# Gated linear attention and a multiplicative FFN: state, scores and values of the last sixteen chunks in one block of 64x64 quarters

## The chip, the cores and the metric

The kernel runs on one core of a Trainium2 chip. The metric is the device time of one execution in microseconds, the median of several runs. All data is float32; TensorE also uses the fp32r form of it, on operands that are split into several parts.

## The reference

An attention layer with a gated state runs over 4 x 8 sequences (batch x heads) of 768 steps with head dimension 48. Its result, laid out as 3072 tokens x 384, goes through a feed-forward network with two factors.

```python
for t in range(S):
    state = alpha[:, :, t, :, None] * state + np.einsum('bhd,bhe->bhde', k[:, :, t], v[:, :, t])
    y[:, :, t] = np.einsum('bhd,bhde->bhe', q[:, :, t], state)
...
x = np.ascontiguousarray(attn_out.transpose(0, 2, 1, 3)).reshape(B * S, H * D)
a = x @ w1            # 384 x 1024
b = x @ w2            # 384 x 1024
h = a * b @ w3        # 1024 x 1024
return (h @ w_out)    # 1024 x 384
```

## The kernel before

**Tiling.** The 3072 tokens are 24 chunks of C = 128, six per sequence (NCH), with all eight heads of a batch entry in one chunk. Heads go in NP = 4 pairs: head 2j lies on partitions 0 to 63 and head 2j + 1 on 64 to 127 (i is 0 or 1; DP = 64 with 48 used). The decays are taken into k and q by sums of logarithms (L324 to L359), so that inside a chunk the scores are plain products. Three chunks (G) make a token group, whose result xd[g] is written to DRAM, read back and multiplied with the FFN weights.

**One chunk.** `transposed` (L370) turns k and q of a chunk on TensorE and ScalarE copies them to qkT (L383). `scores` forms k times q, 128 keys x 128 queries per head, and VectorE masks them with a bitwise and (ms). `attend_state` (L463) multiplies the state T with q into two PSUM banks y; `attend` (L477) adds the values times ms and ScalarE copies y to x (L489), which two DMA transfers write to xd. `outer` (L386) makes the state's new term k times v, `advance` (L405) rescales the state on POOL every second chunk.

**The late chunks.** From chunk TURNED = 8 on, `turned_scores` (L422) leaves out the quarter of each score block that is all masked: keys 0 to 63 for all 128 queries (L430, 128 columns), keys 64 to 127 for queries 64 to 127 (L430, 64 columns), each on 48 rows and 64 columns of the array. For odd heads (i = 1) the two key halves come to lie on exchanged partitions, and `turn_v` (L164) makes POOL copy their values to vt in that order, with the key halves exchanged. Four VectorE instructions mask a chunk (L440). The value products are split: `attend_low` (L415) handles queries 0 to 63 from keys 0 to 63, 64x64 quarters of the array placed between the next chunk's scores, and L482 handles queries 64 to 127 from all 128 keys, after the next chunk's transposes. In scores and y each row half of the array writes a bank of its own.

**Order.** The loop at L689 runs over the chunks: in iteration n stand the state products of chunk n - 1, the scores of chunk n with the low value products of n - 1, the transposes of n + 1, then the masks, the value products of n - 1, the outer products of n, and pieces of the FFN's first stage (`gate`, L515 by way of `exact`). From iteration 9 on an iteration has 3, 3, 2 or no such pieces. The iterations without pieces (9, 13, 17, 21) split the x of a token group into three parts (`split_x`, L507 to L509). Instructions are placed by a scheduling layer; `issue_after` marks hold some of them behind others. Each engine runs its own in its order. PSUM has eight banks, all from one pool (`bank`), which gives out the bank that was given back first.

**Queues.** SP issues the loads of alpha (L147), k and q (L153, L154), v (L159), the weights (L236), and the stores of x (L305) and of the gates (L590). At the head of an iteration `store` empties the list of x transfers, and then come the loads of later chunks: alpha of n + 5, k and q of n + 4, v of n + 2. POOL issues the small transfers of the decays.

After the 24 chunks come the remaining FFN products, the weights w3 times w_out, and the last projection.

Of the kernel before, what the change touches and what calls it, by code (L numbers as in the profile page):

```python
# [48 lines left out]
def kernel(  # L49
# [31 lines left out]
    TURNED = 8  # L81
    assert D <= DP and DM % C == 0 and DF % CW == 0 and S % C == 0 and N % G == 0
# [81 lines left out]
    def turn_v(n):  # L164
        if turned(n):
            for half in range(2):
                nc.gpsimd.tensor_copy(out=vts[n % 2][ds(DP * half, DP), :, 0:D],
                                      in_=st["v", n][ds(DP * (1 - half), DP), 1::2, 0:D])
# [39 lines left out]
    for half in range(2):  # L208
        nc.gpsimd.tensor_copy(out=keep_turned[ds(DP * half, DP), 1 - half], in_=keep[ds(DP * half, DP), ds(DP * half, DP)])
    nc.gpsimd.memset(keep_turned[DP:, 1], -1)  # L210
# [204 lines left out]
    def attend_low(n, jj, i, half):  # L415

        s, w = ds(DP * i, DP), (vts[n % 2] if i else st["v", n])
        h = half * NP // 2 + jj
        nc.tensor.matmul(st["y", n][0][i][ds(DP * half, DP), jj, 0:DP], w[s, h if i else 2 * h, :],  # L419
                         st["ms", n][s, i, h, 0:DP], start=(n % NCH == 0 and jj == 0), stop=True, skip_group_check=True)  # L420

    def turned_scores(n):  # L422

        qkT = st["qkT", n]
        sc = [bank().rearrange("p (j c) -> p j c", j=NP) for _ in range(2)]
        for j in range(NP):
            for part in range(2):
                for i in range(2):
                    r, t = ds(DP * i, D), slice(DP * part, C)
                    nc.tensor.matmul(sc[i][ds(DP * (part ^ i), DP), j, t], qkT[r, 0, j, ds(DP * part, DP)],  # L430
                                     qkT[r, 1, j, t], start=True, stop=True)
            if turned(n - 1):
                for i in range(2):
                    attend_low(n - 1, j % 2, i, i ^ (j < 2))
        ms = work.tile([C, 2, NP, C], FP32, tag="ms", name="ms")
        for i in range(2):
            r = ds(DP * i, DP)
            low, high = (keep_turned[r, 0], keep_turned[:, 1]) if i else (keep[r, 0:DP], keep[:, DP:])
            for x, mask, t in ((slice(DP * i, DP * (i + 1)), low, slice(0, DP)), (slice(0, C), high, slice(DP, C))):
                masked = nc.vector.tensor_tensor(ms[x, i, :, t].bitcast(I32), sc[i][x, :, t].bitcast(I32),  # L440
                                                 mask[:, None, :].to_broadcast([x.stop - x.start, NP, DP]),
                                                 op=ALU.bitwise_and)
        ends_of_part1[0] = mark["ms", n] = masked.ins
        st["ms", n] = ms

    def scores(n):
        if turned(n):
            return turned_scores(n)
# [28 lines left out]
    def attend(n):  # L477
        (y, heads), ms, vc = st.pop(("y", n)), st.pop(("ms", n)), st.pop(("v", n))
        for j, i, to in heads:
            if turned(n):  # L480
                w = vts[n % 2][:, j, :] if i else vc[:, 2 * j, :]
                nc.tensor.matmul(to[:, DP:], w, ms[:, i, j, DP:], start=False,  # L482
                                 stop=(j % HP == HP - 1), skip_group_check=True)
            else:
                nc.tensor.matmul(to, vc[:, 2 * j + i, :], ms[:, i, j, :], start=(n % NCH == 0 and j % HP == 0),  # L485
                                 stop=(j % HP == HP - 1), skip_group_check=True)
# [202 lines left out]
    for n in range(N + 1):  # L689
# [17 lines left out]
        if n:  # L707
            attend_state(n - 1)
# [168 lines left out]
```

## Time and profile before

| | |
|---|---|
| median of 3 runs | 465.62 us (464.9 to 467.0) |
| profiled execution | 464.49 us, its span 462.8 us |
| granted TensorE clock | 1.00 |
| PE busy in the span | 446.9 us, 97% |
| DVE (VectorE) busy | 371.7 us, 80% |
| ACT (ScalarE) busy | 276.4 us, 60% |
| POOL busy | 95.1 us, 21% |
| state products L474 | 320 records, 13.3 us |
| scores of late chunks L430 | 512 records, 34.8 us in two forms |
| low value products L419 | 256 records, 32.8 us in two forms |
| high value products L482 | 256 records, 17.4 us in two forms |

The span is what the profiler saw of the execution; the profiled execution's own time lies 1.7 us above it. Busy times of TensorE are those of overlapping records, whose ends are modelled; the start times of successive groups say more. A float32 matmul is two records of PE and two of PEld (weight load). Late chunks are on TensorE from 67.7 to 184.6 us.

A line of a timeline has start in us, length in us, engine, source line, operation, the tile written and the tiles read, rows x columns of the array in use, the shape of the moving operand, the number of records and, in brackets, the idle time before it with the engine that ended it. A line of a table of groups has the busy time in us and the mean of one in ns, then the idle time before. A line of a table of stages has the window, its length, and for each of PE, PEld, DVE, ACT and POOL the busy time and number of instructions, then the granted clock, the DMA share and GB/s.

### The profile page before, as it was taken

Reading aid. Unit: us, or ns where it says so; the run is one execution under the profiler, and the core shown is the slowest. Engines: PE = TensorE matmul, PEld = TensorE weight load, DVE = VectorE, ACT = ScalarE, POOL = GpSimd, SP = SyncE. Lnnn points to the kernel's source line nnn. Section 1 sums busy time; section 2 is a strip of 40 time slices with the busy share of each in tenths; the row PEclk is TensorE's granted clock in tenths of the full one; section 3 lists DMA queues with packets and bytes.
Section 4 is the critical chain, followed back from the end, with each engine's and each line's share of the span. In section 5 each row is a group of like instructions: output and inputs, shape, how many; then the busy total and the mean of one; then the engine's idle time right before and its main releaser. Section 6 shows DMA issues by size and latency. Waiting matters only on the chain.

```text
span 462.8 us, 11150 instructions
## 1 busy us (share of the span) xinstructions
PE 446.9 (97%) x4296; PEld 423.2 (91%) x4296; DVE 371.7 (80%) x610; ACT 276.4 (60%) x544; POOL 95.1 (21%) x186
## 2 busy tenths in 40 slices
PE   4998999999999999999999999999999999999996
PEld 2675699898999989999999999999999999999996
DVE  2779997999979988999998999997542967776671
ACT  4685975767658563988875676764545443333430
POOL 6234232325414430121221201212010000000000
PEclk9999999999999999999999999999999999999999
DMA  9999999999999974466856446412115875665511
GB/s 173 254 208 228 261 224 192 248 209 219 184 227 193 234 165 138 130 224 212 235 178 196 146 128 177 149 52 86 51 48 153 243 210 180 186 178 159 166 51 52
DMA packets 148869, 80.37 MB, mean 174 GB/s; under 512 B 97392, under 2 KB 138608, under 8 KB 148816
## 3 DMA queue, kind: packets, MB, share of 16 engines
q1 hardware_dynamic: 143040, 64.44, 57.3%
q0 software_dynamic: 5776, 15.22, 11.0%
q8 instruction: 34, 0.56, 0.5%
q14 instruction: 19, 0.16, 0.1%
HBM read 57.58 MB, written 22.06 MB: 172 GB/s over the span
## 4 chain that ended last, share of the span: by engine, by line
PE 88%; DVE 4%; DMA 4%; ACT 2%; issue 1%; SPq 0%; DVEq 0%; ACTq 0%
PE bank L515 72%; DMA kq<-in_q_dram 3%; PE bank L381 3%; PE bank L430 3%; PE bank L482 2%; PE bank L474 2%; PE bank L340 1%; PE bank L393 1%; PE bank L346 1%; PE bank L454 1%; PE bank L343 1%; PE bank L419 1%; DVE qk L359 1%; DVE ms L457 1%; PE bank L485 1%
## 5 line engine op out<-in xcount | busy, mean ns | idle before, releaser
L515 PE MATMUL bank<-x,w 128*128 128x384 f32 x1152 | 210.2, 337 | 1.7 <-ACT qkT L383 1.1
L515 PEld LDWEIGHTS bank<-x,w 128*128 128x128 f32 x1152 | 200.2, 188 | 4.1 <-ACT qkT L383 1.4
L515 PE MATMUL bank<-w3o,ab 128*128 128x384 f32 x576 | 100.2, 336 | 0.0
L515 PEld LDWEIGHTS bank<-w3o,ab 128*128 128x128 f32 x576 | 99.9, 188 | 0.0
L540 ACT ACTIVATE bank<-bank 128x384 f32<-128x384 f32 x96 | 45.6, 476 | 43.4 <-PE bank L515 43.1
L524 ACT ACTIVATE t<-bank 128x384 f32<-128x384 f32 x64 | 31.9, 499 | 54.9 <-PE bank L515 54.9
L590 POOL DMA_DIRECT2D abd<-ab x45 | 25.8, 573 | 137.9 <-DVE ab L576 121.3
L383 ACT COPY qkT<-bank 128x512 f32<-128x512 f32 x48 | 26.2, 596 | 24.8 <-PE bank L381 24.8
L641 DVE TENSOR_TENSOR ab<-abl,ab 128x1024 fp32r<-128x1024 f32 x24 | 29.3, 1223 | 12.3 <-ACT ab L640 12.3
L640 ACT ACTIVATE ab<-abl 128x1024 fp32r<-128x1024 f32 x24 | 25.5, 1061 | 20.2 <-PE bank L515 18.4
L515 PE MATMUL bank<-wo,w3T 128*128 128x384 f32 x192 | 35.9, 334 | 0.0
L576 DVE TENSOR_TENSOR ab<-bank,r 128x384 f32<-128x384 f32 x44 | 24.1, 548 | 12.5 <-PE bank L515 6.3
L515 PEld LDWEIGHTS bank<-wo,w3T 128*128 128x128 f32 x192 | 33.5, 188 | 0.0
L249 ACT ACTIVATE power<-power,rebias 128x512 uint32<-128x512 uint32 (+1 forms) x36 | 25.3, 701 | 12.6 <-DVE power L248 12.4
L359 DVE TENSOR_TENSOR qk<-kq,e 128x768 f32<-128x768 f32 x24 | 23.1, 964 | 11.3 <-ACT e L350 7.9
L526 DVE SCALAR_TENSOR_TENSOR o<-bank,t 128x384 f32<-128x384 f32 x24 | 13.4, 557 | 23.0 <-issue 13.7
L642 DVE SCALAR_TENSOR_TENSOR ab<-ab,abl 128x1024 fp32r<-128x1024 f32 x24 | 29.2, 1217 | 0.0
L526 DVE SCALAR_TENSOR_TENSOR r<-bank,t 128x384 f32<-128x384 f32 x40 | 22.0, 550 | 6.8 <-PE bank L515 3.4
L251 DVE SCALAR_TENSOR_TENSOR mant<-mant,rest 128x512 f32<-128x512 uint32 (+1 forms) x36 | 23.4, 649 | 3.7 <-ACT rest L244 3.7
L252 DVE SCALAR_TENSOR_TENSOR power<-raw,power 128x512 uint32<-128x512 uint32 (+1 forms) x36 | 23.5, 653 | 2.4 <-ACT power L249 2.4
L253 DVE TENSOR_TENSOR mant<-mant,power 128x512 f32<-128x512 f32 (+1 forms) x36 | 23.6, 655 | 0.5
L244 ACT ACTIVATE rest<-raw 128x512 f32<-128x512 uint32 (+1 forms) x36 | 23.3, 649 | 0.0
(102 smaller groups left out, 675.2 us busy)
## 6 DMA issues: line engine op xcount, KB each, us to landing
abl<-abd SPq DMA_DIRECT2D x24, 512.0 KB, 4.7
abd<-ab POOLq DMA_DIRECT2D x45, 192.0 KB, 3.2
raw<-in_moe_w_dram SPq DMA_DIRECT2D x64, 128.0 KB, 3.4
raw<-in_moe_w_dram SPq DMA_DIRECT2D x12, 512.0 KB, 5.8
xT<-xd POOLq DMA_DIRECT2D x9, 576.0 KB, 4.7
kq<-in_k_dram SPq DMA_DIRECT2D x24, 192.0 KB, 5.2
kq<-in_q_dram SPq DMA_DIRECT2D x24, 192.0 KB, 5.4
xd<-x SPq DMA_DIRECT2D x48, 96.0 KB, 3.9
```

What stands on the lines that cost most here:

```text
L249: nc.scalar.activation(power, power, AF.Relu, scale=2.0 ** 23, bias=rebias)
L359: mark["qk", n] = nc.vector.tensor_mul(qks[n % 3][:, :, :, 0:D], st.pop(("kq", n)), st.pop(("e", n)).rearrange("p i (h d) -> p i h d", h=H ...
L383: mark["qkT", n] = nc.scalar.copy(qkT[:, :, :, ds(DP * half, DP)], tp[half]).ins
L515: nc.tensor.matmul(p, w[part][i], x[part][i], start=start and part == parts[0] and i == 0, stop=stop and part == parts[-1] and i == n - 1, ...
L524: nc.scalar.activation(t, p1, AF.Copy, scale=(1.0 + 1.0 / P) * scale)
L526: nc.vector.scalar_tensor_tensor(to, p2, scale, t, op0=ALU.mult, op1=ALU.add)
L540: nc.scalar.activation(p, p, AF.Copy, scale=1.0 + 1.0 / P)
L576: nc.vector.tensor_mul(ab, p, r[0])
L590: (nc.gpsimd if late else nc.sync).dma_start(out=abd[g][:, f, :], in_=ab)
L640: nc.scalar.activation(t[:, 0], ab, AF.Copy, scale=1.0 - 2.0 ** -13)
L641: nc.vector.tensor_sub(t[:, 1], ab, t[:, 0].bitcast(FP32))
L642: nc.vector.scalar_tensor_tensor(t[:, 2], t[:, 0].bitcast(FP32), -1.0 - 1.0 / P, ab, op0=ALU.mult, op1=ALU.add)
```

## The change

For chunks 8 to 23, state, scores and values are put on 64x64 quarters of the array and issued as one block.

- `attention(n)` takes the place of `attend_state(n - 1)` and `turned_scores(n)` at the head of an iteration and merges two lists by the number of columns issued so far. One holds chunk n - 1's state and value products of head pairs 0 to 2 (LQ = 3), on the quarters whose row half and column half differ. The other holds chunk n's scores and then the products of pair 3 of chunk n - 1, on the quarters whose halves agree.
- The scores of both heads of a pair go to the same bank, on the partitions of their half: one bank for keys 0 to 63 and one half-filled for keys 64 to 127. Two masks with 128 partitions take the place of four.
- All value products of chunk n - 1 lie in that block, in three parts per pair (state, keys 0 to 63 for all queries, keys 64 to 127 for queries 64 to 127), so that L482 falls away for these chunks. The value halves that `turn_v` copies are chosen accordingly: its two copies now take even and odd heads.
- y is one bank of 3 x 128 columns and one of 128. Two ScalarE copies of that size take them to x, at the place where `attend` stood; in the scheduled order they now stand ahead of the qkT copies. Four DMA transfers per chunk write x in place of two, of the same bytes in all.
- Chunks 0 to 7 keep their code. Iteration 8 still takes the state of chunk 7 by `attend_state` and its values by `attend`, with the new scores of chunk 8; iteration 24 has the block without scores.

```diff
     TURNED = 8
+    LQ = 3
...
     def turn_v(n):
         if turned(n):
-            for half in range(2):
-                nc.gpsimd.tensor_copy(out=vts[n % 2][ds(DP * half, DP), :, 0:D],
-                                      in_=st["v", n][ds(DP * (1 - half), DP), 1::2, 0:D])
+            for i in range(2):
+                nc.gpsimd.tensor_copy(out=vts[n % 2][ds(DP * i, DP), :, 0:D],
+                                      in_=st["v", n][ds(DP * (1 - i), DP), i::2, 0:D])
 
...
-    for half in range(2):
-        nc.gpsimd.tensor_copy(out=keep_turned[ds(DP * half, DP), 1 - half], in_=keep[ds(DP * half, DP), ds(DP * half, DP)])
-    nc.gpsimd.memset(keep_turned[DP:, 1], -1)
+    for i in range(2):
+        nc.gpsimd.tensor_copy(out=keep_turned[ds(DP * i, DP), 0], in_=keep[ds(DP * i, DP), ds(DP * i, DP)])
+    nc.gpsimd.memset(keep_turned[:, 1], -1)
+    keeps = [keep_turned[:, 0:x, None, :].to_broadcast([C, x, NP, DP]) for x in (1, 2)]
...
-    def attend_low(n, jj, i, half):
-
-        s, w = ds(DP * i, DP), (vts[n % 2] if i else st["v", n])
-        h = half * NP // 2 + jj
-        nc.tensor.matmul(st["y", n][0][i][ds(DP * half, DP), jj, 0:DP], w[s, h if i else 2 * h, :],
-                         st["ms", n][s, i, h, 0:DP], start=(n % NCH == 0 and jj == 0), stop=True, skip_group_check=True)
-
-    def turned_scores(n):
-
+    def quarters(n):
+
+        ms, vc, vt, qkT = st.pop(("ms", n)), st.pop(("v", n)), vts[n % 2], st.pop(("qkT", n))
+        y = [bank()[:, 0:x * C].rearrange("p (j c) -> p j c", c=C) for x in (LQ, NP - LQ)]
+        first, state = set(), n % NCH > 0
+
+        def add(j, i, w, x, t):
+            at = j >= LQ
+            to = y[at][ds(DP * (i if at else 1 - i), DP), j - LQ * at, t]
+            nc.tensor.matmul(to, w, x, start=(at, i) not in first, stop=True, skip_group_check=True)
+            first.add((at, i))
+
+        def steps(heads):
+            for j in heads * state:
+                yield 2, [(j, i, Ts[n % 2][ds(DP * i, D), j, :], qkT[ds(DP * i, D), 1, j, :], slice(0, C)) for i in range(2)]
+            for j in heads:
+                yield 2, [(j, i, vt[DP:, j, :] if i else vc[0:DP, 2 * j, :], ms[ds(DP * i, DP), 0:2, j, :], slice(0, C))
+                          for i in range(2)]
+            for j in heads:
+                yield 1, [(j, i, vc[DP:, 2 * j + 1, :] if i else vt[0:DP, j, :], ms[ds(DP * i, DP), 2, j, :], slice(DP, C))
+                          for i in range(2)]
+
+        def act(x):
+            for y in x:
+                add(*y)
+
+        def copied():
+            x = work.tile([C, NP // 2, 2, C], FP32, tag="x", name="x", bufs=4).rearrange("p j i c -> p (j i) c")
+            for a, b in zip(y, (x[:, 0:LQ], x[:, LQ:])):
+                mark["x"] = ends_of_part1[1] = nc.scalar.copy(b, a).ins
+            g, c = divmod(n, G)
+            to = xd[g].rearrange("(j i d) t -> i d j t", i=2, d=D)[:, :, :, ds(c * C, C)]
+            for half in range(2):
+                s = ds(DP * half, D)
+                later.append((to[1 - half, :, 0:LQ], x[s, 0:LQ]))
+                later.append((to[half, :, LQ:], x[s, LQ:]))
+
+        st["x", n] = copied
+        return *([(k, act, x) for k, x in steps(list(h))] for h in (range(LQ), range(LQ, NP))),
+
+    def quarter_scores(n):
         qkT = st["qkT", n]
-        sc = [bank().rearrange("p (j c) -> p j c", j=NP) for _ in range(2)]
-        for j in range(NP):
-            for part in range(2):
-                for i in range(2):
-                    r, t = ds(DP * i, D), slice(DP * part, C)
-                    nc.tensor.matmul(sc[i][ds(DP * (part ^ i), DP), j, t], qkT[r, 0, j, ds(DP * part, DP)],
-                                     qkT[r, 1, j, t], start=True, stop=True)
-            if turned(n - 1):
-                for i in range(2):
-                    attend_low(n - 1, j % 2, i, i ^ (j < 2))
-        ms = work.tile([C, 2, NP, C], FP32, tag="ms", name="ms")
-        for i in range(2):
-            r = ds(DP * i, DP)
-            low, high = (keep_turned[r, 0], keep_turned[:, 1]) if i else (keep[r, 0:DP], keep[:, DP:])
-            for x, mask, t in ((slice(DP * i, DP * (i + 1)), low, slice(0, DP)), (slice(0, C), high, slice(DP, C))):
-                masked = nc.vector.tensor_tensor(ms[x, i, :, t].bitcast(I32), sc[i][x, :, t].bitcast(I32),
-                                                 mask[:, None, :].to_broadcast([x.stop - x.start, NP, DP]),
-                                                 op=ALU.bitwise_and)
-        ends_of_part1[0] = mark["ms", n] = masked.ins
-        st["ms", n] = ms
+        sc = [bank().rearrange("p (e j c) -> p e j c", e=2, j=NP), bank()[:, 0:NP * DP].rearrange("p (j c) -> p j c", j=NP)]
+
+        def score(x):
+            j, late = x
+            for i in range(2):
+                r, to = ds(DP * i, D), ds(DP * i, DP)
+                q = qkT[r, 1, j, ds(DP * late, DP)] if late else qkT[r, 1, j, :].rearrange("p (e c) -> p e c", e=2)
+                nc.tensor.matmul(sc[1][to, j, :] if late else sc[0][to, :, j, :], qkT[r, 0, j, ds(DP * late, DP)], q,
+                                 start=True, stop=True)
+
+        def masked():
+            ms = st["ms", n] = work.tile([C, 2, NP, C], FP32, tag="ms", name="ms").rearrange("p i j c -> p (i j c)")[:, 0:3 * NP * DP].rearrange(
+                "p (e j c) -> p e j c", e=3, j=NP)
+            for x, y, keep in ((ms[:, 0:2], sc[0], keeps[1]), (ms[:, 2:], sc[1][:, None], keeps[0])):
+                last = nc.vector.tensor_tensor(x.bitcast(I32), y.bitcast(I32), keep, op=ALU.bitwise_and)
+            mark["ms", n] = ends_of_part1[0] = last.ins
+
+        return [(2 - late, score, (j, late)) for j in range(NP) for late in range(2)], masked
+
+    def attention(n):
+
+        low, high = quarters(n - 1) if turned(n - 1) else ([], [])
+        done = None
+        if n < N:
+            own, done = quarter_scores(n)
+            high = own + high
+        low, high, at = deque(low), deque(high), [0, 0]
+        while low or high:
+            k = 0 if not high or low and at[0] <= at[1] else 1
+            cost, f, x = (low, high)[k].popleft()
+            at[k] += cost
+            f(x)
+        if done:
+            done()
 
     def scores(n):
-        if turned(n):
-            return turned_scores(n)
         qkT = st["qkT", n]
         sc = [bank().rearrange("p (j c) -> p j c", j=NP) for _ in range(2)]
         for j in range(NP):
...
         for j, i, to in heads:
-            if turned(n):
-                w = vts[n % 2][:, j, :] if i else vc[:, 2 * j, :]
-                nc.tensor.matmul(to[:, DP:], w, ms[:, i, j, DP:], start=False,
-                                 stop=(j % HP == HP - 1), skip_group_check=True)
-            else:
-                nc.tensor.matmul(to, vc[:, 2 * j + i, :], ms[:, i, j, :], start=(n % NCH == 0 and j % HP == 0),
-                                 stop=(j % HP == HP - 1), skip_group_check=True)
+            nc.tensor.matmul(to, vc[:, 2 * j + i, :], ms[:, i, j, :], start=(n % NCH == 0 and j % HP == 0),
+                             stop=(j % HP == HP - 1), skip_group_check=True)
...
-        if n:
+        if 0 < n <= TURNED:
             attend_state(n - 1)
-        if n < N:
+        if n < TURNED:
             scores(n)
         else:
-            for j in range(NP):
-                for i in range(2):
-                    attend_low(n - 1, j % 2, i, i ^ (j < 2))
+            attention(n)
...
-        if n:
+        if n > TURNED:
+            st.pop(("x", n - 1))()
+        elif n:
             attend(n - 1)
```

## The prediction

> **What bounds the kernel now.** I read the page's busy shares and its chain first, to learn which engine sets the time; then the PE groups by shape, the PE timeline of one late chunk, a table of stages around the chunks that the change touches, and last the waits of PE and of SP.
>
> ```profile
> PE 446.9 (97%) x4296; PEld 423.2 (91%) x4296; DVE 371.7 (80%) x610; ACT 276.4 (60%) x544; POOL 95.1 (21%) x186
> PE 88%; DVE 4%; DMA 4%; ACT 2%; issue 1%; SPq 0%; DVEq 0%; ACTq 0%
> ```
>
> TensorE is busy 97% of the span and carries 88% of the chain. After 188 us, when the last chunk is done, it shows no gap, so time there does not depend on the change. The question is what TensorE does between 68 and 185 us, chunks 8 to 23. One such chunk (iteration 12), with the start and length of each group:
>
> ```profile
> 99.12 0.67 PE L474 MATMUL bank<-qkT,T 48*64 48x128 f32 x16
> 99.61 0.38 PE L430 MATMUL bank<-qkT 48*64 48x128 f32 x7
> ...
> 100.83 0.71 PE L381 MATMUL bank<-ident,qk 64*128 64x64 f32 x16
> 101.47 0.34 PE L482 MATMUL bank<-ms,v 128*64 128x64 f32 x4
> ...
> 101.98 0.62 PE L393 MATMUL bank<-v,qk 128*64 128x48 f32 x16
> ```
>
> State products (L474) take 99.12 to 99.61, scores with the low value products between them (L430, L419) 99.61 to 100.83, transposes to 101.47, the high value products (L482) 101.47 to 101.98. So the parts that change cost 0.49 + 1.22 + 0.51 = 2.22 us in this chunk, and the same stretch of the next iterations agrees within 0.05.
>
> Where TensorE stands still in this stretch, the weight loads show it (the PE rows hide part of it, their ends being modelled):
>
> ```profile
> 86.39 0.30 PEld L515 LDWEIGHTS bank<-x,w 128*128 128x128 f32 x2 [1.42 <-ACT qkT L383]
> 110.06 0.46 PEld L474 LDWEIGHTS bank<-qkT,T 48*64 48x64 f32 x16 [0.60 <-PE bank L346]
> 110.96 0.24 PEld L430 LDWEIGHTS bank<-qkT 48*64 48x64 f32 x8 [0.44 <-ACT w L260]
> 172.46 0.65 PEld L515 LDWEIGHTS bank<-x,w 128*128 128x128 f32 x4 [0.87 <-DVE ms L440]
> ```
>
> These four are 3.33 us together. About 0.2 of each comes at any such place (a change of tiling elsewhere leaves 0.26 between records, a full matmul 0.19), so 2.5 us are real stalls. All follow a chunk in which the x of a token group is split (L507 to L509), where VectorE is full:
>
> ```profile
> 80.00:90.00 10.00, 8.90 (x145) 8.12 (x142) 9.19 (x17) 8.62 (x20) 2.85 (x4) 1.00 0.93 235
> 106.00:110.00 4.00, 3.79 (x100) 3.07 (x98) 3.94 (x10) 3.08 (x6) 1.20 (x4) 1.00 0.99 188
> 110.00:119.00 9.00, 8.68 (x140) 8.08 (x141) 8.94 (x16) 7.01 (x18) 3.37 (x5) 1.00 0.91 215
> ```
>
> The columns after the length are PE, PEld, DVE, ACT and POOL busy, then the granted clock (1.00 throughout): DVE is at 3.94 of 4.00 and 8.94 of 9.00. So PE is the bound, and DVE the second one in the chunks with a split.
>
> **TensorE, step by step.** Each array quarter (row half by column half) works alone. In the trace's single records, those that follow one another in a quarter start 0.109 us apart for 128 columns and 0.059 us for 64, and a float32 matmul is two records: 0.218 and 0.118 us. Test on the chunk above: the fullest quarter has two L474 matmuls (0.436) and four of 128 columns and two of 64 among the scores and low products (1.108): 1.54 against 1.71 measured, so 0.17 for filling and for the change to the transposes' tiling.
>
> After, row half i to column half i (the diagonal) gets all scores, 4 x (0.218 + 0.118) = 1.344, and the products of head pair 3: state 0.218, value 0.218 and 0.118, 0.554. Sum 1.898. The other diagonal gets pairs 0 to 2: 3 x 0.554 = 1.662. They run side by side, so a chunk takes 1.898 + 0.17 = 2.07 against 2.22 before: **-0.15 us**, and the L482 step is gone. The number of matmuls (40) does not change.
> - 13 iterations of this kind (9 to 23 without 13 and 19): 13 x -0.15 = -1.95.
> - Iterations 13 and 19, whose previous chunk began a sequence and has no state: before 1.26 + 0.51 (106.20 to 107.46, then L482); after 1.344 and pair 3 without its state 0.336, 1.68 + 0.17 = 1.85. +0.08 each, +0.16.
> - Iteration 8 has scores of the new form and nothing for the other diagonal: before 1.47 (67.75 to 69.22), after 0.436 + 1.344 + 0.17 = 1.95. +0.48.
> - Iteration 24 has no scores: before 1.50 (183.07 to 184.57), after 1.662 + 0.17 = 1.83. +0.33.
>
> Sum for TensorE's own work: **-1.0 us**. Could the interleaving lose time, since instructions are issued in order? In the stage before, the fullest quarter ran without holes while the other diagonal (0.7 us of 1.1) did not matter; after, both are nearly full. Bounds: none lost, or 0.25 us a chunk, as when each of the two heaviest lists waits once for a 128-column matmul of the other: 15 x 0.25 = +3.8. I take none, because the list is sorted by columns so that both diagonals advance together.
>
> One thing no row shows: L430 and L419 give each row half a bank of its own, while after, both row halves write one bank at once, in different partitions. The bounds are no cost and full turns: 1.898 would become 3.80, +1.9 us in 15 chunks, +28 us. I take no cost, as two column halves of L393 already write one bank's two partition halves together, at 0.62 us for 16 records. The Trainium skill (TensorEngine Tiling (Array Packing), Gotcha 1: PSUM Pressure) speaks against the change here: it says that different row tiles write to different banks and cannot access the same bank simultaneously. By that rule the sum would be the upper end, some 490 us; by the row of L393 it is nothing, and no run shown decides between them yet.
>
> **VectorE.** The four masks of a chunk become two:
>
> ```profile
> L440 DVE TENSOR_TENSOR ms<-bank,keep_turned 64x256 int32<-64x256 int32 x16 | 6.8, 428 | 0.5
> L440 DVE TENSOR_TENSOR ms<-bank,keep_turned 128x256 int32<-128x256 int32 x16 | 6.8, 425 | 0.2
> L440 DVE TENSOR_TENSOR ms<-bank,keep 64x256 int32<-64x256 int32 x16 | 6.5, 408 | 0.0
> L440 DVE TENSOR_TENSOR ms<-bank,keep 128x256 int32<-128x256 int32 x16 | 6.5, 406 | 0.0
> ```
>
> 1.67 us go; a 128x512 mask (L457, 681 ns) and a 128x256 one (425) come: 1.11. -0.56 a chunk, 9 us of VectorE in all. It lies beside TensorE except where TensorE waits for it. At 110 us both waits are for banks that masks of the chunk before release; 0.56 us earlier, and with the first of two masks releasing one of the banks, 0.7 of them goes. At 172.46 the waiting matmuls wanted a scores bank; in the new order the first three of that piece's banks are ones that earlier copies have freed, so 0.7 goes. At 86.39 the bank was held by a qkT copy that stood behind an ACT step waiting for VectorE; the new order gives that matmul a bank of y, copied before. But two pieces later TensorE meets the masks of that chunk (86.71 to 88.95 us, in a VectorE without holes), so I count half, 0.6. Against it: the transposes now start 0.35 us later in a chunk (2.07 against 1.71), and with them the qkT copies and the split, L507 to L509, behind them; the 0.56 of the masks pays for that. **-2.0 us**; bounds 0 and -2.5.
>
> **ScalarE and POOL.** Two copies of 128x256 (377 ns each) become one of 384 and one of 128 columns: by L524 (499 for 384) and the slope to L383 (596 for 512) about 0.50 + 0.27, nothing in sum. They move ahead of the qkT copies, since y is complete before the transposes; they take 0.75 us while the 16 transposes take 0.64, so the qkT copies start 0.1 us late at most, hidden where L515 follows. vt is ready early (the copy for chunk 10 ends at 84.2 us, its first use is at 91.2). POOL's setup writes are one 64x64 block larger, long before chunk 8 reads them. All nothing; without that cover, 0.1 a chunk, +1.6.
>
> **SP.** Each chunk's x goes out in four transfers instead of two, the bytes unchanged.
>
> ```profile
> 103.72 0.91 SPq L305 DMA_DIRECT2D xd<-x  x2
> 104.72 0.41 SPq L147 DMA_DIRECT2D ac<-in_alpha_dram  x1
> 105.18 0.67 SPq L153 DMA_DIRECT2D kq<-in_k_dram  x1
> 105.91 1.32 SPq L154 DMA_DIRECT2D kq<-in_q_dram  x1
> 107.34 0.64 SPq L159 DMA_DIRECT2D v<-in_v_dram  x1
> ...
> 110.27 0.95 SPq L305 DMA_DIRECT2D xd<-x  x2
> ```
>
> Two stores take 0.91 us, so 0.9 more per chunk, 14 us of queue in all, and behind them stand alpha, k, q and v of later chunks. From 68 to 158 us SP's own waits add up to about 13 us over 12 chunks, 1.1 per chunk, part of them for the very copies that now come earlier. So 0.9 just fits. alpha has the least slack: it lands 4.8 us after issue (median), 0 to 3.6 us before its logarithm, and one logarithm waits 1.37 us for it at 116 us. A late alpha stalls ACT, and TensorE only one iteration on. I take **+0.3 us**; bounds 0 and, if no wait of SP could be used, 12 x 0.9 = +10.8.
>
> **Sum.** -1.0 - 2.0 + 0.3 = -2.7. The profiled execution took 464.49 us (span 462.8), 1.1 below the median of 465.62 of the runs shown; -2.7 from the median gives **463 us**.
>
> **Rivals.**
> 1. The gaps stay. The 0.35 us by which qkT and the split come later eats what the masks save; VectorE's 8.94 of 9.00 speaks for it, its idle 0.73 us before L508 at 81 us (it waits for ACT, not for masks) too. Then -1.0 + 0.3: 465. Chance 0.2.
> 2. Slower: SP becomes the bound. Place: alpha and k/q of chunks 12 to 20. It decides once more than 0.2 of the 1.1 us of waits per chunk cannot be used. With half of them usable, 12 x (0.9 - 0.55) = +4.2, less the 1.0 of TensorE and with the gaps as they were: 469. For it: SP is issuing nearly all the time to 158 us; against: its longest issues (q, up to 3.4 us) look like waiting for room, and shrink if others take the time. Chance 0.12.
> 3. The quarters do not fill (+3.8 - 2.7): 467. Chance 0.08.
> 4. The shared bank serialises the row halves (+28): about 490. Chance 0.04.
>
> **How the numbers follow.** The forecast case, PE work and most gaps, has 0.56 and reaches from 461 (all 2.5 of the gaps, some switch saved where L482 was followed by no outer product) to 464.5. Half a per cent, about what a measurement of this kernel can tell from no change, is 2.3 us: the border is at 463.3. Of the 0.56 I put 0.45 below it and 0.11 above; rival 1 lies within; of rivals 2 and 3 0.07 stay within. So faster 0.45, same 0.38, slower 0.17. The range runs from 460.8 to 467.8: it takes in rivals 1 and 3 and half of rival 2. The likeliest case's own range is 461 to 464.5.
>
> **What would show it.** In the profile after: state, scores and values in one group of 2.0 to 2.1 us from the end of the gates to the transposes, no 128*64 value group after chunk 8; two masks of about 680 and 425 ns; x copies ahead of the qkT copies; the stalls near 110 and 172 us gone. A group of 2.3 us or more would show rival 3, one near 3.9 rival 4. Waits of ACT for alpha, or of VectorE for k and q, in several chunks would show rival 2; stalls of the old size after each split, rival 1.

## Result: slower by 0.7%, and the profile after

The changed kernel takes 467.71 us (median of 7 runs), the kernel before 464.54 us (median of 7): a ratio of 1.007, 95% interval 1.0043 to 1.0096. It is slower by 3.2 us, where 463 us and a gain were forecast. The profiled execution shown here took 467.49 us (span 465.8); that of before took 464.49 (span 462.8).

The page of the kernel after: busy time by engine, the granted clock of TensorE in 40 slices, and the chain of waits.

```profile
PE 448.6 (96%) x4296; PEld 426.8 (92%) x4296; DVE 363.3 (78%) x578; ACT 277.9 (60%) x544; POOL 96.0 (21%) x186
PEclk9999999998899999999999999999999999999999
PE 86%; DMA 5%; DVE 3%; ACT 3%; SPq 2%; issue 1%; DVEq 0%; ACTq 0%
```

VectorE lost 8.4 us of work, as the change means it to (371.7 before). But the chain now has 5% of DMA and 2% of SP's queue (4% and 0% before), and two slices of the clock read 8.

The block itself first: TensorE's timeline of the kernel after in iteration 12 (start, length, and the releaser of idle time if any), the counterpart of the chunk shown in the prediction.

```profile
98.23 0.33 PE L426 MATMUL bank<-qkT,T 48*64 48x128 f32 x2
98.24 0.33 PE L466 MATMUL bank<-qkT 48*64 48x128 f32 x2
...
100.28 0.71 PE L383 MATMUL bank<-ident,qk 64*128 64x64 f32 x16
100.93 0.67 PE L395 MATMUL bank<-v,qk 128*64 128x48 f32 x16
101.53 1.67 PE L556 MATMUL bank<-x,w 128*128 128x384 f32 x8
```

State products (L426) and scores (L466) begin 0.01 us apart, so both diagonals run side by side, and the transposes follow at 100.28: 2.05 us. No L482 group stands behind the transposes. The two masks that remain cost what was forecast, by the page's groups by shape:

```profile
L473 DVE TENSOR_TENSOR ms<-bank,keep_turned 128x512 int32<-128x512 int32 x16 | 10.9, 680 | 0.2 <-PE bank L466 0.2
L473 DVE TENSOR_TENSOR ms<-bank,keep_turned 128x256 int32<-128x256 int32 x16 | 6.6, 411 | 0.0
```

The four stalls of TensorE shown for the kernel before (86, 110, 111, 172 us) are gone in this trace. Two others are there. The smaller one is this, in the timeline of the weight loads after:

```profile
94.56 1.51 PEld L556 LDWEIGHTS bank<-x,w 128*128 128x128 f32 x9 [0.95 <-DVE ms L473]
```

The larger one is in iteration 14. Timeline of all engines after:

```profile
110.96 0.71 PE L383 MATMUL bank<-ident,qk 64*128 64x64 f32 x16
...
111.38 3.61 SPq L307 DMA_DIRECT2D xd<-x  x4
...
115.01 0.93 PEld L395 LDWEIGHTS bank<-v,qk 128*64 128x64 f32 x16 [3.47 <-DMA v<-in_v_dram]
115.01 1.10 PE L395 MATMUL bank<-v,qk 128*64 128x48 f32 x16 [3.33 <-DMA v<-in_v_dram]
```

The transposes end at about 111.6 us, and the outer products of chunk 14 (L395; L393 in the kernel before) wait until 115.01 for the values of that chunk. SP's queue shows that they were issued late:

```profile
104.28 1.87 SPq L307 DMA_DIRECT2D xd<-x  x4
106.25 0.40 SPq L148 DMA_DIRECT2D ac<-in_alpha_dram  x1
106.69 0.58 SPq L154 DMA_DIRECT2D kq<-in_k_dram  x1
107.32 1.90 SPq L155 DMA_DIRECT2D kq<-in_q_dram  x1
109.33 0.81 SPq L160 DMA_DIRECT2D v<-in_v_dram  x1
```

Before, v of chunk 14 was issued at 107.34 us, now at 109.33: the queue came 0.56 later to the stores, the four stores take 0.96 more than two, and the q issue 0.58 more; with small changes of the others that is 2.0 us. The transfer itself then took 5.7 us from issue to landing, where it had taken 4.6 before; no run shows why. The stall is not all. The same stretches after, with busy times and then the granted clock (the 0.70, 0.50 and so on ahead of the DMA share):

```profile
106.00:110.00 4.00, 4.00 (x124) 3.56 (x120) 3.43 (x7) 3.50 (x8) 1.32 (x3) 1.00 0.69 130
110.00:119.00 9.00, 5.67 (x87) 5.37 (x79) 6.41 (x9) 4.36 (x11) 4.67 (x7) 0.70 0.88 208
115.00:117.00 2.00, 1.99 (x19) 1.90 (x20) 0.71 (x3) 0.00 (x0) 1.68 (x4) 0.50 0.74 176
119.00:121.00 2.00, 2.00 (x9) 2.00 (x9) 0.56 (x1) 0.26 (x2) 1.00 (x2) 0.65 1.12 204
121.00:124.00 3.00, 3.00 (x44) 2.75 (x46) 2.42 (x4) 2.09 (x5) 1.08 (x3) 1.00 0.99 130
```

The clock falls to half at 113.56 us, while TensorE still waits, and comes back at 120.38 us; full matmuls start 0.32 us apart at half clock and 0.17 to 0.18 apart after it. From the transposes of chunk 15 to those of chunk 16 the kernel after needs 14.36 us, the kernel before 8.87: 5.5 more, of which 3.4 is the wait and the rest, with the forecast 0.15 that the block saves there, some 2.3, is put down to the clock.

To compare traces I use one length throughout: from the start of the transposes of chunk 8 to the end of the span. The code ahead of it is the same in all kernels and came out up to 1.0 us shorter or 0.9 longer from one profiled execution to the next. It is 405.7 us before and 408.8 after.

### The profile page after: what moved, and what is told of

It is laid out like the page before. It is cut to its first block, busy times and chain, and to the rows that moved or that the text cites. A ratio compares the mean times of both kernels' runs of the same rounds, so it can differ in the third digit from the quotient of the medians.

```text
span 465.8 us, 11170 instructions
## 1 busy us (share of the span) xinstructions
PE 448.6 (96%) x4296; PEld 426.8 (92%) x4296; DVE 363.3 (78%) x578; ACT 277.9 (60%) x544; POOL 96.0 (21%) x186
## 4 chain that ended last, share of the span: by engine, by line
PE 86%; DMA 5%; DVE 3%; ACT 3%; SPq 2%; issue 1%; DVEq 0%; ACTq 0%
PE bank L556 71%; PE bank L426 4%; PE bank L383 2%; PE bank L395 2%; DMA kq<-in_q_dram 2%; PE bank L466 2%; DMA v<-in_v_dram 1%; PE bank L500 1%; PE bank L345 1%; PE bank L342 1%; DMA raw<-in_moe_w_dram 1%; SPq L155 1%; DVE qk L361 1%; PE bank L348 1%; PE bank L526 1%
## 5 line engine op out<-in xcount | busy, mean ns | idle before, releaser
L556 PEld LDWEIGHTS bank<-x,w 128*128 128x128 f32 x1152 | 202.3, 189 | 1.9 <-DVE ms L473 1.0
L466 PE MATMUL bank<-qkT 48*64 48x128 f32 (+1 forms) x512 | 24.9, 247 | 0.0
L426 PE MATMUL bank<-ms,v 64*64 64x64 f32 (+1 forms) x256 | 24.4, 244 | 0.0
```

The source lines that it names most:

```text
L426: nc.tensor.matmul(to, w, x, start=(at, i) not in first, stop=True, skip_group_check=True)
L466: nc.tensor.matmul(sc[1][to, j, :] if late else sc[0][to, :, j, :], qkT[r, 0, j, ds(DP * late, DP)], q, start=True, stop=True)
L556: nc.tensor.matmul(p, w[part][i], x[part][i], start=start and part == parts[0] and i == 0, stop=stop and part == parts[-1] and i == n - 1, ...
```

## Experiments

Theory S: the block is worth about what was forecast, and the loss is SP's queue, in which the two extra stores per chunk hold up the loads behind them, v first. Rivals: B, the block is dearer than its sum; D, later T, four smaller transfers cost in the transfer engines, wherever they stand in the queue; L, v is late in the kernel before already; Q, a further cost found on the way, that the scores of two iterations wait for the qkT copies; R, against Q, that these two blocks are long by their order.

### Two stores instead of four

```diff
-            for a, b in zip(y, (x[:, 0:LQ], x[:, LQ:])):
-                mark["x"] = ends_of_part1[1] = nc.scalar.copy(b, a).ins
+            nc.scalar.copy(x[:, 0:LQ], y[0])
+            for i in range(2):
+                mark["x"] = ends_of_part1[1] = nc.scalar.copy(x[ds(DP * (1 - i), DP), LQ:], y[1][ds(DP * i, DP)]).ins
...
-                later.append((to[1 - half, :, 0:LQ], x[s, 0:LQ]))
-                later.append((to[half, :, LQ:], x[s, LQ:]))
+                later.append((to[1 - half], x[s]))
```

> The changed kernel with x written in two transfers per chunk again: ScalarE copies the fourth head pair's two halves across to the other partitions (two copies of 64x128 in place of one of 128x128), so that one transfer per half holds all four pairs. Theory S (the two extra stores on SP hold up the v load of chunk 14): the 3.5 us stall before the outer products of chunk 14 is gone, TensorE's clock stays at 1.00, time 461.5 to 463.5 against 464.5 of the kernel before. Rival D (TensorE now reaches chunk 14 too early for any v load, stores or not): a stall of 2 us or more stays there, 466 to 468. Rival B (the new block or its bank order is at fault elsewhere): 467.

Measured: 463.07 us, ratio to the kernel before 0.9965, interval 0.9949 to 0.9981. The same block with two stores is faster than the kernel before. In the profile of this run the granted clock is 0.85 nearly throughout, so its lengths can't be set beside the others; the kernel was run again:

> The two-store kernel once more, for a profile that is not disturbed and as the base of the run with the scores last. Expected: 462.5 to 463.7 us (ratio 0.995 to 0.998); no wait of the outer products of chunk 14 for v; a block of 2.06 us, and of 2.7 us in iterations 18 and 22. Should v be late in it too, theory S loses its clearest case.

Measured: 464.31 us, ratio 0.9986 (0.9962 to 1.0011). It lies above the 462.5 to 463.7 us expected, and by this run alone it can't be told from no change; the two runs together say a gain between 0.6 and 1.6 us. The trace says clearly what the stores do. SP's queue and TensorE's weight loads in this kernel:

```profile
104.46 0.93 SPq L307 DMA_DIRECT2D xd<-x  x2
...
107.65 0.99 SPq L160 DMA_DIRECT2D v<-in_v_dram  x1
```

```profile
112.90 0.57 PEld L383 LDWEIGHTS bank<-ident,qk 64*128 64x128 f32 x16
113.54 0.55 PEld L395 LDWEIGHTS bank<-v,qk 128*64 128x64 f32 x16
114.14 1.53 PEld L556 LDWEIGHTS bank<-x,w 128*128 128x128 f32 x9
```

v of chunk 14 leaves 1.7 us earlier than in the changed kernel, although the execution runs 1.9 us behind it at that place (transposes of chunk 15 at 112.90 against 110.96), and the outer products follow the transposes without a wait. The length from the transposes of chunk 8 is 404.9 us, 0.8 less than before and 3.9 less than with four stores.

So the half of S that concerns the queue holds, but the block isn't worth what was forecast: of the 3.0 us that the forecast gave to TensorE and VectorE, this trace shows 0.8. Two parts of the rest can be read in it. The block is 0.8 us over its sum in each of iterations 18 and 22 (below), and three stalls stand where the kernel before had four (0.52 us at 88.40, 1.15 at 96.43 and 0.57 at 173.59), so that only 0.9 of the 2.5 us of stalls is saved.

### Four stores in the kernel before

```diff
-            later.append((to[half, :, :, ds(c * C, C)], x[ds(DP * half, D)]))
+            for part in (slice(0, 3), slice(3, 4)) if turned(n) else (slice(0, 4),):
+                later.append((to[half, :, part, ds(c * C, C)], x[ds(DP * half, D), part]))
```

> The kernel before with nothing changed but the stores of chunks 8 to 23: each of the two transfers is cut into one of three head pairs and one of one. Theory S: v, alpha and k/q come 0.9 us later per chunk here too; v of chunk 14 had 1.5 us in hand, so a stall of 0.5 to 3 us, time 465.5 to 469. Rivals D and B: same as the kernel before, within 0.5 us.

Measured: 468.12 us, ratio 1.0086 (1.0058 to 1.0114). The extra stores alone make the old block as slow as the changed kernel. SP's queue, and the lines of the waits for v between 68 and 188 us (in total, times, longest):

```profile
105.21 1.86 SPq L305 DMA_DIRECT2D xd<-x  x4
...
110.43 0.75 SPq L159 DMA_DIRECT2D v<-in_v_dram  x1
```

```profile
PE bank L393 <- DMA v<-in_v_dram: 1.8, 2, 1.4
```

The four stores take 1.86 us as in the changed kernel, v of chunk 14 leaves at 110.43, and L393 waits for it at 113.65 to 115.13 us. Here the clock stayed at 1.00 after the wait of 1.5 us. The length from the transposes of chunk 8 is 2.8 us more than before: 1.4 at this wait, and 1.4 between the transposes of chunks 18 and 20, where the second wait for v takes 0.4 and the rest was not traced. So the stores cost this much without any part of the new block, and B isn't needed for the loss.

### v ahead of the stores

```diff
+        if n > TURNED:
+            load_v(n + 2)
         if not 1 < n < FIRST:
             store()
...
-        if n >= FIRST:
+        if FIRST <= n <= TURNED:
             load_v(n + 2)
```

The same edit was made in the changed kernel, in the one with two stores, and in the kernel before.

> The changed kernel, four stores kept, but from chunk 9 on the v load stands ahead of the stores of its iteration on SP instead of behind stores, alpha, k and q. Theory S: v of chunk 14 is issued some 5 us earlier and the stall goes; alpha, k and q are as late as in the changed kernel, so part of the loss may come back by the alpha logarithm: 462 to 465. Rival B: 467 to 468. Rival D: as theory S, but then e1 keeps its stall.

Measured for the changed kernel with four stores: 464.22 us, ratio 0.9988 (0.9967 to 1.0009). All four transfers are there, only their place in the queue differs, and 3.5 us of the time are gone; so most of the loss is not the transfers themselves. What is late next is alpha, which went back by one v issue. SP's queue, ScalarE and TensorE's weight loads:

```profile
104.16 0.38 SPq L160 DMA_DIRECT2D v<-in_v_dram  x1
104.64 2.08 SPq L307 DMA_DIRECT2D xd<-x  x4
```

```profile
118.04 0.52 ACT L326 ACTIVATE la<-ac 128x384 f32<-128x384 f32 x1 [4.03 <-DMA ac<-in_alpha_dram]
```

```profile
118.99 0.14 PEld L466 LDWEIGHTS bank<-qkT 48*64 48x64 f32 x2 [0.90 <-ACT t L565]
119.58 0.14 PEld L466 LDWEIGHTS bank<-qkT 48*64 48x64 f32 x2 [0.38 <-DVE r L567]
```

The weight loads stand still for 0.90 us and 0.38 us (118.1 to 119.6), where the gates' banks wait behind that logarithm on ScalarE. So with four stores a load that stands behind them is late in either order.

> The changed kernel with two stores per chunk (ScalarE puts pair 3 into the right partitions) and, from iteration 9 on, the value load issued ahead of these stores. Theory S (the time lost is SP's queue: what stands behind the stores is late) expects no wait for v or alpha and the time of the two-store kernel, 462.3 to 463.7 us (ratio 0.995 to 0.998). If v was still late in the two-store kernel, which its disturbed profile could not show, about 461.5 us. Rival T (the number and size of the transfers costs, wherever they stand in the queue) expects nothing from the order either, so this run does not tell S from T, but shows in an undisturbed profile what is left of the forecast gain of 3.0 us: the block at 2.06 us, and the stalls that are still there.

Measured with two stores: 463.6 us, ratio 0.9967 (0.9944 to 0.9989). No wait for v, none of TensorE for alpha, a length of 404.6 us: the same as two stores alone.

> The kernel before, with only the value load issued ahead of the stores from iteration 9 on. Theory S with its slack of 1.5 us at v of chunk 14 (landed about 111.9, used at 113.4 us) expects nothing: 464.2 to 465.3 us (ratio 0.999 to 1.001). Rival L (v is late in the kernel before already, and the gain of the two-store kernel is that of a freer queue rather than of the block) expects 462.5 to 463.5 us (ratio 0.995 to 0.997).

Measured for the kernel before: 464.84 us, ratio 1.0002 (0.9982 to 1.0022). Nothing, as S expects from 1.5 us of slack; L falls: what the two-store kernels gain does not come from an earlier v.

### The stores of pair 3 from POOL's queue

```diff
-            dst, src = later.popleft()
-            nc.sync.dma_start(out=dst, in_=src)
+            dst, src, *pool = later.popleft()
+            (nc.gpsimd if pool else nc.sync).dma_start(out=dst, in_=src)
...
-                later.append((to[half, :, LQ:], x[s, LQ:]))
+                later.append((to[half, :, LQ:], x[s, LQ:], 1))
```

> The changed kernel with its four stores per chunk kept, the two of pair 3 issued from POOL's queue instead of SP's. Theory S expects SP to issue v of chunk 14 at 107.5 to 108.5 us instead of 109.33, no stall of the outer products at 111 us, and 462.5 to 464 us (ratio 0.995 to 0.999). Rival T (four smaller transfers cost in the transfer engines themselves) expects v of chunk 14 to land near 114 to 115 us again and 466 to 468 us (ratio 1.003 to 1.007).

Measured: 468.28 us, ratio 1.0087 (1.0055 to 1.0119): the time is T's, the trace is S's. SP issues v of chunk 14 at 106.07 us, and nothing waits at 112 us; up to the transposes of chunk 21 this execution stands 1.2 us ahead of the kernel before. Then POOL's own queue does what SP's did. Its timeline, and TensorE's weight loads:

```profile
159.87 0.20 POOL L412 TENSOR_TENSOR dec<-dec 128x4 f32<-128x4 f32 x1 [6.07 <-DMA dec<-ends]
...
161.90 1.04 POOL L307 DMA_DIRECT2D xd<-x  x2
163.00 0.50 POOL L414 TENSOR_TENSOR T<-tmp,dec 128x192 f32<-128x192 f32 x1
```

```profile
163.56 0.19 PEld L426 LDWEIGHTS bank<-qkT,T 48*64 48x64 f32 x4 [2.34 <-POOL T L414]
```

The two stores take 1.04 us between the vt copies and the decayed state (L414), which the state products wait for; the wait for the decay factors ahead of them makes POOL late in the first place. 2.3 us of stall, and again half the clock behind it (0.50 from 165 to 167 us); two shorter waits for the vt copies follow (0.37 us at 170.7 and 0.79 at 172.2). My expectation missed because I had counted POOL as free at 21% busy: it stands in waits, and what is queued behind them is on the path.

### v from POOL's queue, with two stores

```diff
-            (nc.gpsimd if 2 < n < 8 else nc.sync).dma_start(out=st["v", n][:, :, 0:D], in_=rows(v, n))
+            (nc.gpsimd if n > 2 else nc.sync).dma_start(out=st["v", n][:, :, 0:D], in_=rows(v, n))
```

> Two stores per chunk, and the value loads of chunks 8 to 23 issued from POOL's queue, so that SP loses 0.64 us per chunk. Theory S expects k, q and alpha to come earlier and no wait for v: 461.5 to 463.5 us (ratio 0.993 to 0.998), at best the full forecast of 3 us. If the queue has no more to give with two stores, the same time as the two-store kernel, 463 us. If POOL waits for v's buffer and holds back its own copies (vt) and decay factors, a new wait of the outer products or of the values for POOL, 464 us or more.

Measured: 465.1 us, ratio 0.9995 (0.9968 to 1.0022); single runs from 462.9 to 468.1. TensorE waits for neither v nor alpha, and nothing is gained over two stores alone. Its profiled execution, the slowest of the run, has a stall of another kind, told below.

### All products off the diagonal

```diff
-    LQ = 3
+    LQ = 4
...
-        y = [bank()[:, 0:x * C].rearrange("p (j c) -> p j c", c=C) for x in (LQ, NP - LQ)]
+        y = [bank()[:, 0:x * C].rearrange("p (j c) -> p j c", c=C) for x in (LQ, NP - LQ) if x]
...
-                later.append((to[1 - half, :, 0:LQ], x[s, 0:LQ]))
-                later.append((to[half, :, LQ:], x[s, LQ:]))
+                later.append((to[1 - half], x[s]))
```

> The changed kernel with all four head pairs' state and value products on the off-diagonal quarters (LQ = 4): y in one bank, one ScalarE copy of 512 columns, two stores per chunk. By the quarter sums the off-diagonal holds 4 x 0.554 = 2.216 us, so the block takes 2.216 + 0.17 = 2.39 us in place of 2.07: +0.32 in 13 chunks, +4 us against e1, 465.5 to 467.5 if theory S holds and e1 is at 462; without the stall at chunk 14. If the block is bound otherwise than by the fullest quarter, it stays near 2.07 and the time near e1.

Measured: 465.78 us, ratio 1.0027 (1.0004 to 1.0049). Two stores come free of charge if all four pairs go off the diagonal, but the fuller diagonal sets a block of 2.36 us in the ordinary iterations, 0.30 more than with LQ = 3 (1.50 in iterations 13 and 19, 0.34 less), and that eats the gain. The quarter sums give both lengths: four times 0.554 and 0.17 are 2.39.

### Scores last in two iterations

In the changed kernel the block takes 2.72 and 2.67 us in iterations 18 and 22, in the two-store kernel 2.89 and 2.87, where other ordinary iterations have 2.05 to 2.15 (and one, iteration 10 with two stores, 2.29). In these two no gate pieces stand between the transposes and the block, and only one other group: 1.19 and 1.24 us from the start of the transposes to the block in the changed kernel. (Iterations 10 and 14 have no pieces either, but two groups and 1.80 us, and blocks of 2.15 and 2.12.) ScalarE of the two-store kernel in iteration 21, and TensorE after it:

```profile
164.97 0.48 ACT L445 COPY x<-bank 128x384 f32<-128x384 f32 x1 [0.95 <-PE bank L426]
165.47 0.54 ACT L447 COPY x<-bank 64x128 f32<-64x128 f32 x2
166.04 1.07 ACT L385 COPY qkT<-bank 128x512 f32<-128x512 f32 x2
```

```profile
165.74 0.67 PE L395 MATMUL bank<-v,qk 128*64 128x48 f32 x16
166.34 0.87 PE L426 MATMUL bank<-qkT,T 48*64 48x128 f32 x12
167.17 0.66 PE L466 MATMUL bank<-qkT 48*64 48x128 f32 x10
```

The qkT copies end at 167.1 and the scores start at 167.17; the scheduling layer, which puts six state products of the low list ahead of them, has only those for cover. In the kernel before L482, L393 and L474 stood there, from 165.57 to 167.13 us, and covered the same copies.

```diff
-            high = own + high
+            high = high + own if n in (18, 22) else own + high
```

> The two-store kernel; in iterations 18 and 22 alone the merged list has the products of head pair 3 ahead of the scores. In the profiles so far the block takes 2.06 us in all its ordinary iterations but 2.72 and 2.67 us in these two, where no pieces of the FFN stand between the transposes and the block. Theory Q (there the scores wait for the qkT copies, which L482 covered in the kernel before) expects the block at 2.05 to 2.15 us in both iterations and 1.0 to 1.3 us less than the two-store kernel of the same call: about 461.9 us where that has 463.1 (ratio to before 0.993 to 0.996). Rival R (the length is that of the issue order or of the two row halves, not of a wait) expects 2.6 to 2.7 us again and no change of the time.

Measured: 464.35 us, ratio 0.9975 (0.995 to 1.0), and 464.31 us for the two-store kernel of the same call: the medians show no difference. The trace shows the block at 2.34 and 2.31 us where the two-store kernel has 2.89 and 2.87: 1.1 us gained there, three quarters of what the block lengths named by Q would give, since the scores still start with the end of the copies (165.03 after 164.97). The profiled execution, 461.76 us with a length of 403.9, is the fastest of its run, so Q is shown in the trace and R falls, but a gain of time isn't shown. Two stores leave little slack: in this trace the outer products of chunk 14 wait 0.2 us for v.

> Two stores, the value load ahead of them, and the scores last in iterations 18 and 22. Theory Q expects 1.0 to 1.3 us less than the kernel with two stores and the value load first (ratio 0.9967 in its call): ratio 0.993 to 0.996, about 462 us. If the time of these runs is set by stalls that come and go from one execution to the next, 463 to 464 us and an interval that reaches 0.998.

Measured: 464.32 us, ratio 0.9979 (0.9956 to 1.0002). The same blocks, 2.34 and 2.31, and no gain that the times can tell from the others. The versions with LQ = 3 and two stores lie between 0.9965 and 0.9995 of the kernel before, against 1.007 for the changed one: 3.5 to 4.9 us less than that, and at most 1.6 less than before.

## Why the prediction was wrong

By its own steps:

1. **TensorE's own work, -1.0: right in size per block, wrong in two iterations.** Measured against forecast: 2.05 to 2.06 us for 2.07 in eight of the twelve ordinary iterations from 9 to 22, 2.12 and 2.15 in two more; 1.84 for 1.85 in iterations 13 and 19, 1.94 for 1.95 in iteration 8, 1.81 for 1.83 in iteration 24. The quarters fill, and rival 3 falls. Iterations 18 and 22 cost 0.4 and 0.65 us more than forecast from transposes to transposes. The step that failed is the one on ScalarE: "the qkT copies start 0.1 us late at most, hidden where L515 follows". They do start on time (141.60 in iteration 17, when the transposes are done), but where L515 doesn't follow, their own length of 1.07 us is no longer covered: L482 had helped to cover it. The bound of 0.1 a chunk counted only the late start. So about 0 in place of -1.0.
2. **VectorE and the gaps, -2.0: right in this trace.** The four stalls are gone (2.5 us of excess over the usual 0.2 at such a place), one of 0.8 came at 94 us: -1.8. Some of that may be the wait at 115 us, in which VectorE can catch up: without it, in the trace with two stores, the saving is 0.9.
3. **The shared bank, 0 within 0 to +28: right.** Both row halves write one bank and the block takes its quarter sum. The Trainium skill (TensorEngine Tiling (Array Packing), Gotcha 1: PSUM Pressure) says that different row tiles cannot access one bank simultaneously. This case doesn't agree: 2.05 us for a block of which that would have made 3.8.
4. **SP, +0.3 within 0 to +10.8: this term was mis-sized, and it decided the sign.** The price of the stores was right (0.96 us for 0.9), the place was not. It named alpha as the load with the least slack and looked at v only by way of vt, whose first use comes an iteration later. But the outer products read v itself. In the trace of before, POOL's copy shows v of chunk 14 landed at 111.92 and L393 starts at 113.41: 1.5 us of slack.

```profile
111.92 2.07 POOL L167 COPY vt<-v 64x192 f32<-64x192 f32 x2 [3.47 <-DMA v<-in_v_dram]
113.41 0.62 PE L393 MATMUL bank<-v,qk 128*64 128x48 f32 x16
```

   After, v lands at 115.01, 3.1 later. And its reader could start at 111.6, 1.8 earlier, because the stalls at 110 us and L482 are gone. 3.1 + 1.8 - 1.5 = 3.4, the wait measured. A good part of this step's loss is thus the gain of steps 1 and 2 run up against a load that came no earlier. With the clock behind it, +5.6 in place of +0.3. The room in the queue was not the fault: the prediction's 13 us cover only the longest of SP's waits between 68 and 158 us, and all of them add up to 17.6, 1.5 per chunk. What counts is the slack of each load at its first reader, not the sum of the queue's waits.

Sum: 0.0 - 1.8 + 5.6 = +3.8, against +3.1 in the two traces and +3.2 in the medians; the 0.7 between is spread over the iterations in pieces of 0.1 to 0.3 and isn't explained further.

Rival 2 had the right mechanism and nearly the right time (469), at 0.12. That the time fits is in part luck: it spread the loss over alpha and k/q of chunks 12 to 20, 0.35 us each, where in the profiled execution it was one load of one chunk, v, and the half clock behind it. Its strongest sign, "SP is issuing nearly all the time to 158 us", stood in the prediction and deserved the higher chance. Rival 4 falls. Rival 1 falls for this trace; with two stores most of the gaps' excess is still there (1.6 of 2.5 us).

How often v of chunk 14 is this late in executions without a profile isn't known. The seven runs after lie between 467.4 and 470.3 us, all above the slowest of the seven before (467.0), so none seems to have escaped the loss. It need not come in the same parts: the profiled execution has a mean clock of 0.992, but two of the seven are at 0.999 and 1.000 and took 468.68 and 468.31 us, a loss without a half clock of that length.

## What to carry to other kernels

When a change adds transfers to a queue that issues nearly all the time, list for every load behind them when it lands and when each of its readers, not just one, would first use it; then subtract what the change itself saves ahead of that reader, because a faster engine eats the slack from the other side. When a group of instructions is moved away, look for the copy that it covered in the iterations where nothing else stands in its place. And an engine that is 21% busy is no free queue if the rest is waiting in order.

## What the runs showed of the hardware

**A stall can cost more than its length.** By the idle time of the weight loads in the late chunks, the granted clock stayed at 1.00 with stalls of 1.42 (before), 1.43 (v first, four stores), 1.48 (before with four stores) and 1.97 us (scores last, v first). It fell to 0.50 with 1.56 (before with v first), 2.27 (v on POOL), 2.34 (stores on POOL) and 3.47 us (after). So the length alone doesn't decide. Up to the end of the last matmuls, half clock always lasts 3.41 or 6.83 us, once or twice the same length, and it doesn't start with the end of the stall: after, it starts 1.5 us ahead of that end; in before with v first, whose stall ends at 83.59, at 85.41. In the kernel with the scores last and v first, clock changes stand at 36.67 and 43.50; counted on in steps of 3.41 us, a boundary falls at 84.46, inside its stall of 1.97 us (83.67 to 85.63). The stalls of 1.56, 2.27 and 2.34 us each lie whole between two such boundaries. How much idle time in one step is enough, the runs don't show: 1.43 and 1.48 us whole in one step left the clock alone.

The kernel with v on POOL, behind its stall of 83.41 to 85.68 us:

```profile
85.68 0.20 PEld L426 LDWEIGHTS bank<-ms,vt 64*64 64x64 f32 x4 [2.27 <-issue]
...
85.70:88.00 2.30, 2.30 (x36) 2.06 (x37) 1.99 (x5) 1.61 (x4) 0.00 (x0) 0.56 0.70 137
88.00:90.00 2.00, 2.00 (x13) 1.91 (x12) 1.93 (x5) 1.04 (x3) 1.15 (x3) 0.50 0.64 122
```

The Trainium skill (TensorE: Matmul & The Clock Gate, Part 1: The HAM clock gate) states that the clock is halved after an idle window of about 3.4 us, and that the window is free-running, so that the time of a change depends on where in it the matmuls fall. The traces agree on the half clock, on the length of the steps and on the chance in it (1.97 us without, 1.56 with), but show the half clock with stalls well under 3.4 us.

**A stall beside a late transfer of instructions.** In five of thirteen profiled executions, one of them of the kernel before with v first, TensorE's weight loads stood still for 1.43 to 2.27 us in iteration 10, with "issue" as the only releaser, as in the line above. The trace also has a 16 KB transfer of the instruction queue near that place. In the eight executions without the stall it starts 0.15 to 1.0 us after the transposes of chunk 10, in the five with it 2.6 to 3.8 us after, and each of these stalls ends 2.2 to 2.5 us after that transfer's start. That the one causes the other is argued from these times, not shown by an experiment; nor do the runs show why the transfer is late, or whether this is what spreads the unprofiled times over 3 to 5 us.
